# A new start for the first head pairs: P turned on VectorE, matrices built in halves, k and v in fp32 by SyncE, and a changed order of loads

## The chip, the cores and the metric

The kernel runs on one core of one Trainium2 chip. The metric is the device time of one execution in microseconds (us). Each run is repeated, and the mean TensorE clock that the core was granted is recorded with each execution.

A run also leaves a profile of one execution. Its span is about 2 us shorter than the device time, since it goes only from the first to the last instruction. Times inside a profile are counted from the start of its span. A load "lands" when its data has arrived.

## The reference

Attention over blocks comes first: a soft permutation P of the eight blocks of each head, found by five rounds of normalisation, sorts k and v. A feed-forward network (FFN) with a squared relu follows.

```python
batch, n_heads, seq, head_dim, n_blocks = 4, 8, 768, 64, 8
P = sort_net                                     # (4, 8, 8, 8)
for _ in range(5):
    P = exp(P - max(P, -1)); P /= sum(P, -1); P /= sum(P, -2)
k_sorted = einsum('bhij,bhjcd->bhicd', P, k in blocks of 96 rows)
v_sorted = einsum('bhij,bhjcd->bhicd', P, v in blocks of 96 rows)
attn = softmax(q_block @ k_sorted_block.T / 8)   # inside each block
x = (attn @ v_sorted).reshape(3072, 512)
out = maximum(x @ w_in, 0)**2 @ w_out            # 512 -> 2048 -> 512
```

## The kernel before

The kernel doesn't emit instructions as its source lists them. It collects operations (`plan.add(engine, estimated cost, function, dependencies)`) and a planner sorts them by the time at which each could start. Each engine then gets its own list and takes it strictly in order. That holds for the loads too: all loads that turn fp32 into bf16 are issued by GpSimd, one after another.

```python
    def dma(key, mb, dst_src, deps=(), long=True, rate=0.23):
        def issue(e):
            dst, src = dst_src()
            nc.gpsimd.dma_start(out=dst, in_=src)
        op = plan.add("POOL", 0.75, issue, deps)          # GpSimd
        landed[key] = plan.add("DMA", mb / (...), lambda e: None, [op, landed.get("last")])
        landed["last"] = landed[key]
    # [cut]
    for g in range(HP):                    # k and v of batch 0, pair of heads by pair
        load(0, 1, 2 * g, 2)
        load(0, 2, 2 * g, 2)
        if g == 0:
            plan.add("POOL", 1.5, make_mask, [id_op])
    load_w_in(0)
    for g in range(1, 4):
        load_w_in(g)
    load(1, 2, 0, HP)                      # "vb": the first half of v of batch 1
    for g in range(4):
        dma(("w_out", g), 1.05, ...)
    for t, g in ((2, 1), (1, 0), (0, 0), (1, 1), (0, 1)):
        load(1, t, HP * g, HP)
```

For the first pairs of batch 0, P is turned by a TensorE transpose, spread over the partitions by small matmuls, and multiplied with a mask on VectorE into the sorting matrices `w_all`. The start is then a fixed list of stages: K and V sort k and v of a pair, S computes scores, T turns v, A applies the attention, X turns the result into `xT` for the FFN.

```python
FIRST = ("K0 V0 K1 v1 S0 t0 S1 k2 t1 A0 V2 S2 K3 t2 A1 V3 X0 A2 S3 t3 x1 A3 X2 x3")
    # [cut]
    pe = plan.add("PE", 0.12, p_trans, [step] + old)
    op = plan.add("DVE", 0.18, lambda e: nc.vector.tensor_copy(out=p_ij, in_=tiles["pT"]), [pe])
    # [cut: spreading]
    build_w(2, 2, pt, cp)
    build_w(4, 4, pt, cp)
```

The softmax here doesn't subtract the row's maximum and nothing guards it: scores larger than these inputs give would overflow.

## Time and profile before

| | kernel before |
|---|---|
| time, median | 224.44 us (223.84 to 224.87, 4 runs) |
| span of the profile, mean clock | 222.0 us, 1.000 |
| TensorE, ScalarE, VectorE, GpSimd busy | 96%, 54%, 46%, 12% |
| first sort of a pair | 12.98 us |
| first FFN matmul | 22.48 us |
| first sort of vb, after 40 FFN matmuls | 30.34 us, no wait |
| second sort of vb | 42.89 us, 0.21 us of waiting |
| wait for vblk (v of a later batch, written to memory and read back) | 1.06 us, ending at 157.23 us |

Lines of a timeline read: start, duration, engine, source line, operation, output<-inputs, shape, count. In brackets stands how long the engine was idle before and what ended the idleness. The prediction shows the main lines of this profile.

### The profile page before, as it was taken

To read this page: it belongs to the slowest core of one execution; us is meant where nothing else is said; L and a number is where in the kernel's file an instruction comes from. 1 tells how busy PE (TensorE), PEld (TensorE's weight loads), DVE (VectorE), ACT (ScalarE), POOL (GpSimd) and SP (SyncE) were. 2 spreads that over 40 slices of the span, in tenths; PEclk is the share of its full clock that TensorE was granted. 3 is DMA by queue.
4 is the path that set the end of the run, shared out by engine and by line. 5 is a ranking of instruction groups with operands and counts; after the bars stand their busy time and mean duration, and the time that the engine had idled before them with its cause. 6 is when DMAs were issued, how large, how long until landed. Compare 5 with 4: busy or idle time off the path is not lost.

```text
span 222.0 us, 5101 instructions
## 1 busy us (share of the span) xinstructions
PE 213.3 (96%) x2049; PEld 120.0 (54%) x2065; DVE 102.8 (46%) x291; ACT 120.8 (54%) x249; POOL 26.5 (12%) x49
## 2 busy tenths in 40 slices
PE   8998999999999999999999999999899999999993
PEld 2576666456665555445665465445555465455562
DVE  6768477444773347602676056404655155015300
ACT  4666888217976168517864178329573276147421
POOL 7973230000000600000000240000000000000000
PEclk9999999999999999999999999999999999999999
DMA  5999999998533499189943599648982510120012
GB/s 68 201 202 207 209 206 214 209 259 229 156 82 80 90 227 223 25 218 223 206 111 83 120 176 218 128 139 177 238 175 68 118 49 3 47 94 0 3 63 78
DMA packets 46583, 31.22 MB, mean 141 GB/s; under 512 B 26016, under 2 KB 41632, under 8 KB 46560
## 3 DMA queue, kind: packets, MB, share of 16 engines
q0 software_dynamic: 12736, 13.63, 37.2%
q1 hardware_dynamic: 33824, 17.27, 30.8%
q8 instruction: 16, 0.26, 0.5%
q14 instruction: 7, 0.06, 0.1%
HBM read 29.70 MB, written 8.72 MB: 173 GB/s over the span
## 4 chain that ended last, share of the span: by engine, by line
PE 75%; DMA 17%; POOL 4%; ACT 1%; issue 1%; DVE 1%; SPq 0%; ACTq 0%
PE op L921 33%; PE hp L893 31%; DMA vb<-in_v_dram 9%; DMA w_in_bf<-in_moe_w_in_dram 5%; PE p L631 3%; PE p L814 3%; DMA vblk<-v_way 2%; PE op L955 2%; PE p L714 2%; POOL vb L300 1%; POOL kb L300 1%; DMA p_sb<-in_sort_net_dram 1%; ACT h L901 1%; DVE h L904 1%; PE qtp L511 0%
## 5 line engine op out<-in xcount | busy, mean ns | idle before, releaser
L893 PE MATMUL hp<-xT,w_in_bf 128*128 128x384 bf16 x512 | 88.9, 326 | 0.0
L921 PE MATMUL op<-w_out_bf,h 128*128 128x512 bf16 x352 | 83.3, 379 | 0.9 <-issue 0.2
L904 DVE TENSOR_TENSOR h<-h 128x384 bf16<-128x384 bf16 x128 | 44.5, 356 | 62.7 <-ACT h L901 62.3
L901 ACT ACTIVATE h<-hp 128x384 bf16<-128x384 f32 x128 | 61.6, 495 | 19.1 <-PE hp L893 15.6
L893 PEld LDWEIGHTS <-w_in_bf 128*128 128x128 bf16 x512 | 48.1, 98 | 32.1 <-issue 1.0
L921 PEld LDWEIGHTS <-h 128*128 128x128 bf16 x368 | 34.0, 98 | 37.6 <-issue 0.9
L229 ACT COPY ob<-op 128x512 f32<-128x512 f32 (+1 forms) x24 | 13.6, 567 | 62.4 <-PE op L921 59.8
L825 DVE TENSOR_TENSOR ao<-p,rec 96x512 bf16<-96x512 f32 x32 | 22.0, 687 | 1.2
L663 ACT ACTIVATE et<-p 96x384 bf16<-96x384 f32 x48 | 19.5, 489 | 3.1 <-PE p L631 3.1
L814 PEld LDWEIGHTS <-et 96*128 96x128 bf16 x256 | 11.3, 97 | 5.5 <-issue 1.7
L824 DVE RECIPROCAL rec<-p 96x8 f32<-96x8 f32 x32 | 6.4, 199 | 16.4 <-PE p L814 16.2
L1047 POOL COPY held<-xT 1x3 bf16<-1x3 bf16 (+1 forms) x2 | 0.4, 183 | 89.2 <-DMA xT<-ao 89.2
L397 PE MATMUL p<-ones 128*128 128x512 bf16 (+1 forms) x36 | 10.0, 399 | 1.1 <-DVE ones L250 1.1
L814 PE MATMUL p<-vblk,et 96*128 96x65 bf16 x192 | 8.9, 193 | 1.1 <-DMA vblk<-v_way 1.1
L231 DVE CAST vn<-p 128x768 bf16<-128x768 f32 x6 | 5.7, 958 | 8.5 <-PE p L714 8.5
L631 PEld LDWEIGHTS <-kx 64*128 64x128 bf16 x160 | 6.1, 156 | 3.9 <-issue 3.7
L631 PE MATMUL p<-qT,kx 64*128 64x96 bf16 x160 | 7.4, 228 | 0.0
L231 DVE CAST kn<-p 128x768 bf16<-128x768 f32 x5 | 4.8, 957 | 4.8 <-PE p L714 4.8
L300 POOL DMA_DIRECT2D kb<-in_k_dram x10 | 6.4, 643 | 3.5 <-DMA w_in_bf<-in_moe_w_in_dram 2.0
L300 POOL DMA_DIRECT2D qb<-in_q_dram x8 | 6.1, 770 | 4.9 <-DMA w_out_bf<-in_moe_w_out_dram 2.1
L300 POOL DMA_DIRECT2D vb<-in_v_dram x10 | 6.3, 628 | 3.3 <-DMA w_in_bf<-in_moe_w_in_dram 2.0
L654 ACT ACTIVATE et<-p 96x768 bf16<-96x768 f32 x8 | 6.2, 804 | 0.1
(80 smaller groups left out, 112.9 us busy)
## 6 DMA issues: line engine op xcount, KB each, us to landing
out_dram<-ob SPq DMA_DIRECT2D x23, 256.0 KB, 2.2
qb<-in_q_dram POOLq DMA_DIRECT2D x8, 384.0 KB, 11.0
v_way<-vn SPq DMA_DIRECT2D x6, 396.0 KB, 4.2
vblk<-v_way SPq DMA_DIRECT2D x6, 396.0 KB, 4.1
vb<-in_v_dram POOLq DMA_DIRECT2D x6, 384.0 KB, 11.4
kb<-in_k_dram POOLq DMA_DIRECT2D x6, 384.0 KB, 10.0
w_in_bf<-in_moe_w_in_dram POOLq DMA_DIRECT2D x4, 512.0 KB, 11.8
w_out_bf<-in_moe_w_out_dram POOLq DMA_DIRECT2D x4, 512.0 KB, 18.9
```

The source lines that it names most:

```text
L229: nc.scalar.copy(out=out, in_=in_)
L231: nc.vector.tensor_copy(out=out, in_=in_)
L300: nc.gpsimd.dma_start(out=dst, in_=src)
L397: nc.tensor.matmul(out=out, lhsT=ones, rhs=rhs, start=True, stop=True)
L631: nc.tensor.matmul(out=scp[:, h, BLK * n:BLK * (n + 1)], lhsT=(u.ksT[64 * h:64 * (h + 1), HS * hf + BLK * n:HS * hf + BLK * n + 128] if no ...
L663: nc.scalar.activation(out=et[:, h, 0:HS].rearrange("p (n c a) -> p n c a", c=C0, a=NA), in_=st["p"][0:96, h, 0:HS].rearrange("p (n a c) - ...
L814: nc.tensor.matmul(out=oup[:, h, 66 * n:66 * n + D + 1], lhsT=et_r[u.et[hf]][:, h, BLK * n:BLK * n + 128], rhs=(u.vs[:, NQ * hf + n, h, 0: ...
L825: nc.vector.tensor_tensor(out=u.ao[:, n0:n0 + NQ, :, :].rearrange("p n e d -> p e n d"), in0=ov[:, :, :, 0:D], in1=rec[:, :, :, None].to_b ...
L893: nc.tensor.matmul(out=t["hp", nt][:, 0:HS], lhsT=w_in_bf[:, kc, 128 * nt:128 * (nt + 1)], rhs=xT[:, kc, t0:t0 + HS], start=(kc == 0), sto ...
L901: nc.scalar.activation(out=t["h1", nt], in_=t["hp", nt][:, 0:HS], func=AF.Relu)
L904: nc.vector.tensor_tensor(out=t["h2"][:, nt, :], in0=t["h1", nt], in1=t["h1", nt], op=ALU.mult)
L921: nc.tensor.matmul(out=t["op", mt], lhsT=t["h2"][:, nt, 128 * mt:128 * (mt + 1)], rhs=w_out_bf[:, nt, :], start=(nt == 0), stop=(nt == NT ...
```

## The change

The intent is an earlier start. P takes a shorter way to the sorting matrices, the first matrix is built only as far as it is needed at once, the first k and v use DMA time that was idle, and nine FFN matmuls go one at a time into gaps of TensorE. To free VectorE, three builds move to GpSimd, and the later loads are put into a function that is called after the builds. One of them, vb, is given the last build as a dependency.

```diff
-FIRST = ("K0 V0 K1 v1 S0 t0 S1 k2 t1 A0 V2 S2 K3 t2 A1 V3 X0 A2 S3 t3 x1 A3 X2 x3")
+FIRST = ("K0' v0 k1 V1 S0 t0 v2 S1 t1' A0 K2' K3 V3 A1 t2 S2 x0' t3' S3 A2 F0 F1 X1' A3 X2' "
+         "F2 F4 F5 F3 x3 F6 F7 F8")
@@ loads
+    kv_f = xT[:, :, 3 * S:].bitcast(FP32).rearrange("p (t h) x -> p t h x", t=2)
+    for t, x in enumerate((k_r, v_r)):
+        nc.sync.dma_start(out=kv_f[:, t], in_=x[0, :, 0:2, :])
-    for g in range(HP):
+    plan.add("POOL", 1.5, make_mask, [id_op])
+    for g in range(1, HP):
         load(0, 1, 2 * g, 2)
         load(0, 2, 2 * g, 2)
-        if g == 0:
-            plan.add("POOL", 1.5, make_mask, [id_op])
-    load(1, 2, 0, HP)
-    for g in range(4):
-        dma(("w_out", g), ...)
+    def loads_after(deps):
+        load(1, 2, 0, HP, deps=deps)
+        for g in range(4):
+            dma(("w_out", g), ...)
@@ P
-        nc.tensor.transpose(
-            out=tiles["pT"], in_=pf.rearrange("h i j -> h (i j)"), identity=ident[0:NH, 0:NH])
+        nc.vector.transpose(out=p_ij.rearrange("p k h -> p (k h)"),
+                            in_=pf.rearrange("h i j -> h (i j)"))
@@ casts and builds
+    def cast(e, t):
+        nc.scalar.copy(out=qkv[0][t][:, 0:2, :], in_=kv_f[:, t - 1])
+    there = plan.add("WAY", 4.8, lambda e: None)
+    for t in (1, 2):
+        landed[0, t, 0, 0] = plan.add("ACT", 0.83, lambda e, t=t: cast(e, t), [there, exps[t]])
-    build_w(2, 2, pt, cp)
-    build_w(4, 4, pt, cp)
+    build_w(2, 2, pt, cp, 0, NQ)
+    builds = [build_w(h0, 4, pt, cp, i0, NQ, "POOL") for h0, i0 in ((4, 0), (0, NQ), (4, NQ))]
+    loads_after(builds[-1:])
@@ single FFN matmuls: stage F in FIRST
+        kc, nt = n // 3, n % 3
+        nc.tensor.matmul(
+            out=tiles["hp", nt][:, 0:HS], lhsT=w_in_bf[:, kc, 128 * nt:128 * (nt + 1)],
+            rhs=xT[:, kc, 0:HS], start=(kc == 0), stop=False)
[cut: the shapes for the turned P, the choice of PSUM buffers (the quote marks in FIRST), planning costs, fill sizes]
```

More of the change, by code (lines that the diff above doesn't have):

```diff
@@ L92 @@
 class Plan:
-    TAIL = {"PE": 0.0, "ACT": 0.09, "DVE": 0.06, "POOL": 0.0, "DMA": 0.0, "SP": 0.0, "WAY": 0.6}
+    TAIL = {"PE": 0.12, "ACT": 0.09, "DVE": 0.06, "POOL": 0.0, "DMA": 0.0, "SP": 0.0, "WAY": 0.6}
     HOP = 0.06
@@ L105, in add @@
     def add(self, eng, cost, fn, deps=(), due=0, ffn=False, mode="full"):
+        if eng == "PE":
+            cost += self.TAIL["PE"]
         op = Op(eng, cost, fn, deps, due, mode)
@@ L312, in in_tiles, with load @@
         return b > 1 and t > 0 or b == 1 and t == 2 or b == 1 and t == 1 and h0 == HP
-    def load(b, t, h0, n, p=slice(0, 128)):
+    def load(b, t, h0, n, p=slice(0, 128), deps=()):
         def dst_src():
@@ L321, in load @@
         dma((b, t, h0, p.start), 1.57 * n / H * (p.stop - p.start) / 128, dst_src,
-            readers[b - 2] + [holds[b]] if b > 1 else [],
+            readers[b - 2] + [holds[b]] if b > 1 else list(deps),
             b < 2 and (b < 1 or in_tiles(b, t, h0)), 0.23 if b == 1 else 0.37 if t else 0.29)
@@ L327, in load_w_in @@
         dma(("w_in", g), 1.05, lambda: (w_in_bf[:, :, f], w_in_r[:, :, f]))
-    first = plan.add("DMA", 4.3, lambda e: None)
+    first = plan.add("DMA", 4.8, lambda e: None)
     landed["last"] = first
@@ L356 @@
         load_w_in(g)
-    load(1, 2, 0, HP)
-    for g in range(4):
-        t = slice(NT // 4 * g, NT // 4 * (g + 1))
-        dma(("w_out", g), 1.05, lambda t=t: (w_out_bf[:, t, :], w_out_r[:, t, :]))
-    for t, g in ((2, 1), (1, 0), (0, 0), (1, 1), (0, 1)):
-        load(1, t, HP * g, HP)
+    def loads_after(deps):
+        load(1, 2, 0, HP, deps=deps)
+        for g in range(4):
+            t = slice(NT // 4 * g, NT // 4 * (g + 1))
+            dma(("w_out", g), 1.05, lambda t=t: (w_out_bf[:, t, :], w_out_r[:, t, :]))
+        for t, g in ((2, 1), (1, 0), (0, 0), (1, 1), (0, 1)):
+            load(1, t, HP * g, HP)
     rs = const.tile([NH, NB], FP32)
@@ L367 @@
     pf = const.tile([NH, NB, NB], BF16)
-    sel = const.tile([64, 64, C0], BF16)
+    sel = const.tile([32, 32, C0], BF16)
     pt = const.tile([128, NB, NH], BF16)
-    p_ij = const.tile([64, NH], BF16)
+    p_ij = const.tile([NH, 2, NH], BF16)
     def sink_norm(e, axis, last=False):
@@ L384, in make_sel @@
         nc.scalar.copy(
-            out=sel, in_=ident[0:64, 0:64, None].to_broadcast([64, 64, C0]))
+            out=sel, in_=ident[0:32, 0:32, None].to_broadcast([32, 32, C0]))
     tiles = {}
@@ L412, with p_turn @@
         if it == 0:
-            plan.add("ACT", 0.9, make_sel, [step, id_op])
+            plan.add("ACT", 0.6, make_sel, [step, id_op])
         step = plan.add("DVE", 0.66, lambda e: sink_norm(e, 0), [step])
         step = plan.add("DVE", 0.69, lambda e, it=it: sink_norm(e, 1, it == 4), [step])
-    def p_trans(e):
-        tiles["pT"] = ps1.tile([64, NH], BF16, tag="p1", name="pT")
-        nc.tensor.transpose(
-            out=tiles["pT"], in_=pf.rearrange("h i j -> h (i j)"), identity=ident[0:NH, 0:NH])
+    def p_turn(e):
+        nc.vector.transpose(out=p_ij.rearrange("p k h -> p (k h)"),
+                            in_=pf.rearrange("h i j -> h (i j)"))
     def p_spread(e, name, n):
@@ L428, in p_spread, with build_w @@
                 out=tiles[name][:, i, :],
-                lhsT=sel[:, NB * i:NB * (i + 1), :].rearrange("p j c -> p (j c)"),
-                rhs=p_ij[:, 0:n], start=True, stop=True)
+                lhsT=sel[:, NB * (i % 4):NB * (i % 4 + 1), :].rearrange("p j c -> p (j c)"),
+                rhs=p_ij[:, i // 4, 0:n], start=True, stop=True)
     built = {}
-    def build_w(h0, n, src, dep):
+    def build_w(h0, n, src, dep, i0=0, ni=NB, eng="DVE"):
+        i1 = slice(i0, i0 + ni)
         def fn(e):
-            s = tiles["pt_01"] if src is None else src
-            nc.vector.tensor_tensor(
-                out=w_all[:, h0:h0 + n, :, :],
+            (nc.vector if e == "DVE" else nc.gpsimd).tensor_tensor(
+                out=w_all[:, h0:h0 + n, i1, :],
                 in0=(mask if h0 < H else mask_1)[:, None, None, :]
-                .to_broadcast([128, n, NB, C0]),
-                in1=s[:, :, h0:h0 + n].rearrange("p i h -> p h i")[:, :, :, None]
-                .to_broadcast([128, n, NB, C0]),
+                .to_broadcast([128, n, ni, C0]),
+                in1=(tiles["pt_01"] if src is None else src)
+                [:, i1, h0:h0 + n].rearrange("p i h -> p h i")[:, :, :, None]
+                .to_broadcast([128, n, ni, C0]),
                 op=ALU.mult)
-        op = plan.add("DVE", 0.15 + 0.134 * n, fn, [dep])
+        cost = 0.15 + 0.134 * n * ni / NB if eng == "DVE" else 0.2 + 0.32 * n * ni / NB
+        op = plan.add(eng, cost, fn, [dep])
         for h in range(h0, h0 + n):
-            built[h] = op
+            for i in range(i0, i0 + ni):
+                built[h, i] = op
         return op
@@ L543, in s_q, with s_sort @@
         return op
-    def s_sort(u, t, due=0, early=False, eng=AD):
+    def s_sort(u, t, due=0, early=False, eng=AD, own=False):
         st = {}
@@ L551, in mm @@
             if early:
-                tp = psf.tile([128, 512], FP32, tag="pf", name="tp")
+                tp = ((ps1 if own else psf)
+                      .tile([128, 512], FP32, tag="p1" if own else "pf", name="tp"))
                 tp = tp[:, 0:NA * u.ni * C0].rearrange("p (a x) -> p a x", a=NA)
@@ L577, in s_sort @@
         dep = landed[u.b, t, h0 if u.b == 0 else HP * (h0 // HP), 0]
-        ring = rf if early else r2
+        ring = (r1 if own else rf) if early else r2
         s2, old = ring.take()
         pe = plan.add("PE", 0.336 if u.full else 0.2, mm,
-                      [dep, built[H * u.b + h0], built[H * u.b + h0 + 1]] + old, due, mode="col")
+                      [dep, built[H * u.b + h0, u.i0], built[H * u.b + h0 + 1, u.i0]] + old, due, mode="col")
         readers[u.b].append(pe)
@@ L608, in s_sort2 @@
         pes = [plan.add("PE", 0.2, lambda e, t=t: mm(e, t),
-                        [landed[u.b, t, 2 * u.hp, 0], built[H * u.b + 2 * u.hp],
-                         built[H * u.b + 2 * u.hp + 1]] + old, due, mode="col") for t in (1, 2)]
+                        [landed[u.b, t, 2 * u.hp, 0], built[H * u.b + 2 * u.hp, u.i0],
+                         built[H * u.b + 2 * u.hp + 1, u.i0]] + old, due, mode="col") for t in (1, 2)]
         readers[u.b] += pes
@@ L669, in s_sc, with s_vt @@
                 u.exps[hf].append(op)
-    def s_vt(u, due=0, eng=AD):
+    def s_vt(u, due=0, eng=AD, own=True):
         st = {}
+        ring = r1 if own else rf
         def mm(e):
-            st["p"] = vbp = ps1.tile([128, u.ni, 128], BF16, tag="p1", name="vbp")
+            st["p"] = vbp = ((ps1 if own else psf)
+                             .tile([128, u.ni, 128], BF16, tag="p1" if own else "pf", name="vbp"))
             for n in range(u.ni):
@@ L686, in ev @@
                  st["p"][0:96].rearrange("p n (e d) -> p n e d", d=D))
-        s1, old = r1.take()
+        s1, old = ring.take()
         pe = plan.add("PE", 0.446 if u.full else 0.22, mm, [u.v_op] + old, due)
         u.vs_op = one_of(eng, cost_b(128 * u.ni), ev, [pe] + u.old)
-        r1.use(s1, pe, u.vs_op)
+        ring.use(s1, pe, u.vs_op)
         rks.use(u.n, pe)
@@ L842, in s_av, with s_xt @@
         u.nao = nao
-    def s_xt(u, due=0, eng=AD):
+    def s_xt(u, due=0, eng=AD, own=True):
         if u.b > 1 or u.b == 1 and u.hp < HP - 1:
@@ L857, in s_xt @@
         st = {}
+        ring = r1 if own else rf
         def mm(e):
-            st["p"] = xtp = ps1.tile([128, u.ni, BLK], BF16, tag="p1", name="xtp")
+            st["p"] = xtp = ((ps1 if own else psf)
+                             .tile([128, u.ni, BLK], BF16, tag="p1" if own else "pf", name="xtp"))
             for n in range(u.ni):
@@ L869, in ev @@
             copy(e, xT[:, u.hp, t0:t0 + BLK * u.ni], st["p"].rearrange("p n q -> p (n q)"))
-        s1, old = r1.take()
+        s1, old = ring.take()
         pe = plan.add("PE", 0.342 if u.full else 0.17, mm, u.norms + old, due)
         op = one_of(eng, cost_b(BLK * u.ni), ev, [pe])
-        r1.use(s1, pe, op)
+        ring.use(s1, pe, op)
         rao.use(u.nao, pe)
@@ L877, in s_xt, with f_piece, mm @@
             x_done[u.b, u.hp, hf] = op
+    begun, f_slot = {}, {}
+    def f_piece(n):
+        kc, nt = n // 3, n % 3
+        def mm(e):
+            if kc == 0:
+                tiles["hp", nt] = psf.tile([128, 512], FP32, tag="pf", name="hp")
+            nc.tensor.matmul(
+                out=tiles["hp", nt][:, 0:HS], lhsT=w_in_bf[:, kc, 128 * nt:128 * (nt + 1)],
+                rhs=xT[:, kc, 0:HS], start=(kc == 0), stop=False)
+        old = begun.setdefault((0, nt), [])
+        if kc == 0:
+            f_slot[nt], old = rf.take()
+        pe = plan.add("PE", 0.163, mm, [x_done[0, kc, 0], landed["w_in", 0]] + old)
+        rf.use(f_slot[nt], pe)
+        begun[0, nt].append(pe)
     def ffn_unit(g):
@@ L890, in up @@
                     t["h2"] = ffn.tile([128, NT, HS], BF16, tag="h2", name="h2")
-                t["hp", nt] = psf.tile([128, 512], FP32, tag="pf", name="hp")
-                for kc in range(KC):
+                kcs = range(len(begun.get((g, nt), ())), KC)
+                if kcs[0] == 0:
+                    t["hp", nt] = psf.tile([128, 512], FP32, tag="pf", name="hp")
+                else:
+                    t["hp", nt] = tiles["hp", nt]
+                for kc in kcs:
                     nc.tensor.matmul(
@@ L905, in square @@
                     out=t["h2"][:, nt, :], in0=t["h1", nt], in1=t["h1", nt], op=ALU.mult)
-            sf, old = rf.take()
-            pe = plan.add("PE", 0.65, up, xs + [landed["w_in", nt // 4]] + old, ffn=True)
+            n = len(begun.get((g, nt), ()))
+            sf, old = rf.take() if n == 0 else (f_slot[nt], begun[g, nt])
+            pe = plan.add("PE", 0.65 * (KC - n) / KC, up, xs + [landed["w_in", nt // 4]] + old, ffn=True)
             s1, old1 = rh1.take()
@@ L976 @@
     q2ops = [s_q(0, hp, 64, 128, after=exps[4], eng="ACT") for hp in range(HP)]
-    s1, old = r1.take()
-    pe = plan.add("PE", 0.12, p_trans, [step] + old)
-    op = plan.add("DVE", 0.18, lambda e: nc.vector.tensor_copy(out=p_ij, in_=tiles["pT"]), [pe])
-    r1.use(s1, pe, op)
+    op = plan.add("DVE", 0.2, p_turn, [step])
     sf, old = rf.take()
     pe = plan.add("PE", 0.25, lambda e: p_spread(e, "pt_01", 2), [op] + old)
-    w0 = build_w(0, 2, None, pe)
+    w0 = build_w(0, 2, None, pe, 0, NQ)
     rf.use(sf, pe, w0)
@@ L997 @@
         stage = stage.upper()
+        if stage == "F":
+            f_piece(n)
+            continue
         if n not in us:
@@ L1001 @@
         u = us[n]
+        own = (name[2:] == "'") ^ (stage in "TX")
         if stage == "K":
-            u.k_op = s_sort(u, 1, early=True, eng=eng)
+            u.k_op = s_sort(u, 1, early=True, eng=eng, own=own)
         elif stage == "V":
-            u.v_op = s_sort(u, 2, early=True, eng=eng)
+            u.v_op = s_sort(u, 2, early=True, eng=eng, own=own)
         elif stage == "S":
@@ L1008 @@
         elif stage == "T":
-            s_vt(u, eng=eng)
+            s_vt(u, eng=eng, own=own)
         elif stage == "A":
@@ L1012 @@
         else:
-            s_xt(u, eng=eng)
+            s_xt(u, eng=eng, own=own)
     n_up = NT + 4 * (HS // 128)
@@ L1074 @@
             if filled and not started and op.gap > 0.15 and slot is not None:
-                fill(op.gap, slot)
+                fill(op.gap - 0.15, slot)
             filled = True
```

## The prediction

> **What bounds the kernel now.** I read the page first: engine shares, then the span in slices.
>
> ```profile
> PE 213.3 (96%) x2049; PEld 120.0 (54%) x2065; DVE 102.8 (46%) x291; ACT 120.8 (54%) x249; POOL 26.5 (12%) x49
> ...
> PE   8998999999999999999999999999899999999993
> ...
> DMA  5999999998533499189943599648982510120012
> ```
>
> TensorE is busy nearly throughout, so the work removed anywhere else is worth only what it lets TensorE start earlier. The third row shows a second limit: for the first nine slices (each 5.55 us) the DMA engines are full as well. In that stretch an early TensorE can run into data that has not come.
>
> Next the timeline of TensorE from 22 to 44 us:
>
> ```profile
> 22.48 0.34 PE L893 MATMUL hp<-xT,w_in_bf 128*128 128x384 bf16 x1
> ...
> 27.81 2.60 PE L893 MATMUL hp<-xT,w_in_bf 128*128 128x384 bf16 x15
> 30.34 0.38 PE L714 MATMUL p<-vb,w_t 32*32 32x384 bf16 x16
> 30.66 1.47 PE L893 MATMUL hp<-xT,w_in_bf 128*128 128x384 bf16 x8
> ...
> 42.89 0.39 PE L714 MATMUL p<-vb,w_t 32*32 32x384 bf16 x16 [0.21 <-DMA vb<-in_v_dram]
> ```
>
> The FFN begins at 22.48; what comes before is the start-up that the change rebuilds. At 30.34, after 40 FFN matmuls, TensorE sorts the first half of v of batch 1 (vb), at 42.89 the second half, which had only just landed. TensorE takes its list in order, so either sort can stop everything behind it.
>
> Last, the timeline of GpSimd, which issues all loads that cast:
>
> ```profile
> 10.42 3.04 POOL L300 DMA_DIRECT2D w_in_bf<-in_moe_w_in_dram  x4
> 14.81 0.55 POOL L300 DMA_DIRECT2D vb<-in_v_dram  x1 [1.35 <-DMA kb<-in_k_dram]
> 15.34 1.54 POOL L300 DMA_DIRECT2D w_out_bf<-in_moe_w_out_dram  x2
> 17.08 0.74 POOL L300 DMA_DIRECT2D w_out_bf<-in_moe_w_out_dram  x1 [0.20 <-issue]
> 19.63 0.74 POOL L300 DMA_DIRECT2D w_out_bf<-in_moe_w_out_dram  x1 [1.81 <-DMA w_in_bf<-in_moe_w_in_dram]
> 22.33 0.54 POOL L300 DMA_DIRECT2D vb<-in_v_dram  x1 [1.96 <-DMA w_in_bf<-in_moe_w_in_dram]
> ```
>
> Two things are to be seen. GpSimd idles before issues until an older load lands: in the program's list each such load waits for the one eight places before it. And vb, needed at 30.34, goes out ahead of all four parts of w_out, which are needed from 37.62 on. Adding the time to landing (view of the load line, one issue at a time) to the start gives the landings: k of pair 2 14.6, v of pair 2 14.9, k of pair 3 15.9, v of pair 3 16.8, the parts of w_in 19.3, 22.1, 24.6, 27.4, vb 28.9, w_out 31.5, 34.0, 37.0, 40.7, second vb 42.8. So vb is only 1.4 us early today, and a part of w_in or w_out takes about 2.6 us of a full DMA.
>
> **What the Trainium skill says.** "DMA: Bandwidth & Descriptors", section "Issuing engines are not separate DMA queues": loads issued by SyncE run on the same 16 engines. The trace agrees that only idle time can be won: the DMA share is 0.29 from 2 to 3 us and 0.84 from 3 to 4, then 1.31 from 5 to 15. The same page, "Two DMAs through the same engine are not ordered": descriptors of a queue start in order. The landings above are in issue order without exception. "GPSIMD Engine Reference", section "3.1 Elementwise — side-by-side cycle accounting": about 2.6 cycles an element against 1 on VectorE. The folds of the mask agree: 64 columns 0.34 us, 16 columns 0.22, so 2.5 ns a column. "TensorE: Matmul & The Clock Gate", section "What's actually happening": after an idle window of about 3.4 us the array runs at half clock until about 3.4 us of work. The trace shows the slow state at the start, where 12 filling matmuls of 512 columns take 5.30 us (0.44 each) against 0.82 for three later (0.27); PEclk doesn't show it.
>
> **The change part by part.**
>
> 1. P is turned on VectorE instead of by a TensorE transpose and a copy. Before: last write of P ends at 11.14, copy of the turned P ends at 11.90. After: one VectorE instruction on 32x64; small VectorE operations here take 0.17 to 0.25, so about 0.2 plus 0.05. Gain 0.5 us.
> 2. The first matrix is built for four of eight blocks. Three builds (256, 256, 512 columns) take 1.56; an estimate for 128 columns is 0.28 against 0.42. Gain 0.15. Pair 0 could be sorted at about 12.3 instead of 12.98.
> 3. k and v of pair 0 come in fp32 by SyncE from about 1.2 us and fill DMA time that was idle. Until 4.5 us the DMA moved 0.16 MB, where 0.2 MB/us is its later rate: about 1.2 us of idle time is filled, so all later landings come about 1.2 us earlier: k of pair 3 at 14.7, the last w_in at 26.2. ScalarE pays two casts of 128x768, 0.80 each by the casts of that shape here; they lie between the exponentials of P, which leave it idle 1.50 before the third.
> 4. Nine FFN matmuls (0.163 each, 1.47 in all) go into gaps of the last pairs, in place of filling matmuls.
> 5. The builds for pairs 2 and 3 move to GpSimd, and the vb load is made to wait for them. This is the part that decides. In the changed program GpSimd's list is: w_in x4, w_out x3, three builds, w_out, vb, vb. The third w_out waits for the eighth load before it, k of pair 3, about 14.7; with 0.74 of issue and a build of 256 columns (0.18 + 256 x 2.5 ns = 0.82) the sort of v of pair 2 starts at about 16.4.
>
> From 16.4 I follow the changed order by hand with durations of this trace: exponential of pair 1 ends 17.9 (0.81), three ScalarE evacuations of 0.48 to 19.4, two exponentials to 21.0, last normalisation (0.19 + 0.69) to 22.3, its transpose and copy (0.2 + 0.36) to about 22.9. At 22.9 nine FFN matmuls are done, so this equals a start at 21.4: a gain of 1.1 us over 22.48, although the first pair gained only 0.65.
>
> Then the loss. The first sort of vb stands behind 36 FFN matmuls instead of 40. From 22.48 to 30.34 there were 7.86 us with 40; with 27 left to do it is 7.86 - 13 x 0.163 = 5.7, so TensorE is there at about 28.6. The vb load is now behind four parts of w_out: 26.2 + 4 x 2.6 + 1.5 (vb's own time, 27.4 to 28.9) = 38.1. **TensorE waits 9.5 us**, with all later work behind it. The sort starts at 38.1 instead of 30.34: 7.8 later. Four more FFN matmuls are still to do: +0.65. The second vb lands at about 41.6, well before its sort, so the old wait there (0.2 to 0.4) goes: -0.3. After 9.5 us of idleness some 3.4 us of work at half clock lose about 1.5. Sum: 7.8 + 0.65 - 0.3 + 1.5 = +9.6 on TensorE's chain. From there to the end TensorE is full, so it goes through to the end: 224.6 + 9.6 = 234.2. I take 233.5, as small waits later (1.1 us for vblk near 157) may shrink and the clock loss is the softest term.
>
> **The rivals.** *The start-up gain comes through*: vb is there in time and the kernel ends 1 to 3 us sooner, 221.5 to 223.5. For it: the 1.1 us above. Against it: the order of loads is fixed in the program, and 4.2 MB at the measured 0.4 MB/us can't pass in the 2.4 us between 26.2 and 28.6. *GpSimd's builds become the bound instead*: if the third w_out is held longer or VectorE's two-input work slows the builds to 1.5 us each, pair 2 is sorted at 17.5 or later and the FFN starts later; but this only shortens the later wait for vb by as much, so the end moves little. *The casts hold up P*: if k of pair 0 lands after 5.0 us, the third exponential is late and all of the start-up with it. Likewise hidden behind vb. *The DMA is faster without the writes to v_way from 31.9 us on*: w_out parts took 3.0 and 3.7 us there and vb could land at 37: 1 us less, about 232.
>
> **Range and chances.** The landing of vb (36.5 to 40) gives 1.5 us each way, the clock 0 to 1.7, the changed order later 1 us each way: 229.5 to 237.5. Slower by over 2% means above 229.1. Even with vb at 36.5 and no clock loss the sum is +6.5, 231.1. Faster by 2% would need 220.1, more than the whole start-up gain: 0.02. Within 2% only if I misread the order: 0.06. Slower: 0.92.
>
> **What the changed profile would show.** Right: a TensorE gap of 8 to 10.5 us ending near 38 at the first sort of vb, put down to the DMA of vb; the fourth w_out issued before vb; first builds on GpSimd near 15.6; the first sort at about 12.3; slow matmuls just after the gap; about 1.1 us gained in FFN matmuls done by 22.9. Wrong: vb landing before 31, or FFN matmuls filling the gap, or GpSimd not waiting at the third w_out.

## The result, and the profile after

The changed kernel took 233.5 us (median, 233.46 to 234.2, 4 runs) against 224.44 us. The ratio is 1.041, with a 95% interval of 1.038 to 1.044: slower. Ratios here are the mean time of one kernel's runs over that of the other's runs of the same rounds, so not quite the ratio of the medians. The changed kernel's profiled span is 231.7 us, with a mean clock of 0.963.

The page of the changed kernel, engine shares and slices of 5.79 us:

```profile
PE 216.5 (93%) x2050; PEld 120.6 (52%) x2050; DVE 102.7 (44%) x292; ACT 121.0 (52%) x249; POOL 26.9 (12%) x50
...
PE   8699762999999999999999999999999999999993
...
PEclk9759995899999999999999999999999999999999
DMA  6999999964326149946994669937996520111012
```

TensorE has one new hole, the seventh slice (digit 2, 34.8 to 40.5 us) with two thinner ones ahead of it (7 and 6), and a thin second slice (digit 6). The clock row is down to 7 and 5 in the second and third slice, and to 5 and 8 in the hole and the slice after it. The DMA row is full right through the hole: the loads don't pause, they bring something else than what TensorE wants.

The timeline of TensorE around the hole, then that of GpSimd:

```profile
29.33 3.42 PE L931 MATMUL hp<-xT,w_in_bf 128*128 128x384 bf16 x20
38.97 0.55 PE L725 MATMUL p<-vb,w_t 32*32 32x384 bf16 x16 [6.21 <-DMA vb<-in_v_dram]
39.45 2.74 PE L931 MATMUL hp<-xT,w_in_bf 128*128 128x384 bf16 x8
...
52.44 0.38 PE L725 MATMUL p<-vb,w_t 32*32 32x384 bf16 x16
```

```profile
13.26 0.74 POOL L306 DMA_DIRECT2D w_out_bf<-in_moe_w_out_dram  x1 [0.23 <-DMA kb<-in_k_dram]
...
15.96 1.84 POOL L443 TENSOR_TENSOR w_all<-mask,pt 128x256 bf16<-128x256 bf16 x3
17.75 0.80 POOL L306 DMA_DIRECT2D w_out_bf<-in_moe_w_out_dram  x1
19.38 0.54 POOL L306 DMA_DIRECT2D vb<-in_v_dram  x1 [0.82 <-DMA w_in_bf<-in_moe_w_in_dram]
```

GpSimd issues three parts of w_out, the builds, the fourth part, and only then vb. TensorE is done with the work ahead of vb at 32.76 and stands for 6.21 us.

The chain of waits that ended last, its two longest early pieces:

```profile
8.98 10.11 DMA w_in_bf<-in_moe_w_in_dram
19.38 19.55 DMA vb<-in_v_dram
```

From 8.98 to 38.93 us the chain consists of transfers and of the issue between them. TensorE is nowhere on it in that time, so whatever the start-up won or lost in those 30 us isn't on the path that set the end.

That start-up did not go as intended. These lines are from the timelines of the kernel before (TensorE, ScalarE, VectorE), then of the changed one:

```profile
6.60 0.91 PE L511 MATMUL qtp<-ident,qb 64*64 64x64 bf16 x36 [0.24 <-DMA qb<-in_q_dram]
7.66 0.26 ACT L409 ACTIVATE p_sb<-p_sb 32x64 f32<-32x64 f32 x1
10.93 0.21 DVE L377 TENSOR_TENSOR pf<-p_sb,cs 32x64 bf16<-32x64 f32 x1
12.98 0.38 PE L560 MATMUL tp<-w_all,kb 128*64 128x64 bf16 x12 [0.25 <-ACT pt L988]
```

```profile
7.99 0.83 ACT L1013 CAST vb<-xT 128x768 bf16<-128x768 f32 x1 [1.69 <-DMA xT<-in_v_dram]
8.14 1.13 PE L519 MATMUL qtp<-ident,qb 64*64 64x64 bf16 x36 [2.05 <-DMA qb<-in_q_dram]
9.10 0.25 ACT L414 ACTIVATE p_sb<-p_sb 32x64 f32<-32x64 f32 x1
12.37 0.21 DVE L382 TENSOR_TENSOR pf<-p_sb,cs 32x64 bf16<-32x64 f32 x1
12.61 0.23 DVE L425 STREAM_TRANSPOSE p_ij<-pf 32x64 bf16<-32x64 bf16 x1
15.28 0.53 PE L569 MATMUL tp<-w_all,kb 128*64 128x64 bf16 x12 [0.22 <-DVE w_all L443]
```

The first q lands at about 8.1 instead of 6.5 us, the fourth exponential of P starts 1.44 us later, and the first sort comes at 15.28 instead of 12.98. Each matmul group of the last line also takes 0.53 instead of 0.38 us: TensorE runs at half clock there. The table of windows of the changed kernel shows where that began (columns: window, its length, then busy time of TensorE, its weight loads, VectorE, ScalarE, GpSimd, then clock, DMA share, GB/s):

```profile
6.00:8.00 2.00, 0.09 (x1) 0.00 (x0) 1.27 (x7) 0.27 (x2) 2.00 (x4) 1.00 1.27 224
8.00:10.00 2.00, 1.85 (x51) 1.53 (x51) 0.55 (x3) 2.00 (x5) 1.79 (x3) 0.56 1.31 202
...
16.00:18.00 2.00, 2.00 (x53) 1.59 (x48) 1.22 (x3) 1.50 (x3) 2.00 (x4) 0.50 1.25 206
```

So two causes offer themselves for the 9.7 us: the late vb, and the late start. The experiments part them.

### The profile page after: what moved, and what is told of

Same layout as the page of the kernel before. It is cut to its first block, busy times and chain, and to the rows that moved or that the text cites. A ratio compares the mean times of both kernels' runs of the same rounds, so it can differ in the third digit from the quotient of the medians.

```text
span 231.7 us, 5097 instructions
## 1 busy us (share of the span) xinstructions
PE 216.5 (93%) x2050; PEld 120.6 (52%) x2050; DVE 102.7 (44%) x292; ACT 121.0 (52%) x249; POOL 26.9 (12%) x50
## 4 chain that ended last, share of the span: by engine, by line
PE 79%; DMA 15%; POOL 3%; issue 1%; DVE 0%; ACT 0%; SPq 0%; POOLq 0%; ACTq 0%
PE op L960 34%; PE hp L931 33%; DMA vb<-in_v_dram 8%; DMA w_in_bf<-in_moe_w_in_dram 4%; PE p L825 3%; PE p L640 3%; DMA vblk<-v_way 2%; PE p L725 2%; PE op L994 2%; POOL kb L306 1%; POOL vb L306 1%; POOL qb L306 0%; PE xtp L876 0%; DVE vn L234 0%; PE p L605 0%
## 5 line engine op out<-in xcount | busy, mean ns | idle before, releaser
L960 PE MATMUL op<-w_out_bf,h 128*128 128x512 bf16 x368 | 84.9, 379 | 0.0
L939 ACT ACTIVATE h<-hp 128x384 bf16<-128x384 f32 x128 | 61.3, 495 | 20.2 <-PE hp L931 16.8
L931 PEld LDWEIGHTS <-w_in_bf 128*128 128x128 bf16 x503 | 47.4, 98 | 33.2 <-issue 3.1
L402 PE MATMUL p<-ones 128*128 128x512 bf16 (+1 forms) x22 | 8.5, 537 | 1.1 <-DVE ones L253 1.1
L725 PE MATMUL p<-vb,w_t 32*32 32x384 bf16 x96 | 2.7, 359 | 6.2 <-DMA vb<-in_v_dram 6.2
L232 ACT CAST vn<-p 128x768 bf16<-128x768 f32 x6 | 4.8, 799 | 6.8 <-PE p L725 6.8
L725 PEld LDWEIGHTS <-w_t 32*32 32x32 bf16 x176 | 1.7, 88 | 10.3 <-issue 9.8
```

The costliest lines, as they stand in the source:

```text
L232: nc.scalar.copy(out=out, in_=in_)
L402: nc.tensor.matmul(out=out, lhsT=ones, rhs=rhs, start=True, stop=True)
L725: nc.tensor.matmul(out=p2[slot][32 * c:32 * (c + 1), h, 0:NA * D], lhsT=w[r, :], rhs=src[r, g, NA * D * c:NA * D * (c + 1)], start=True, s ...
L931: nc.tensor.matmul(out=t["hp", nt][:, 0:HS], lhsT=w_in_bf[:, kc, 128 * nt:128 * (nt + 1)], rhs=xT[:, kc, t0:t0 + HS], start=(kc == 0), sto ...
L939: nc.scalar.activation(out=t["h1", nt], in_=t["hp", nt][:, 0:HS], func=AF.Relu)
L960: nc.tensor.matmul(out=t["op", mt], lhsT=t["h2"][:, nt, 128 * mt:128 * (mt + 1)], rhs=w_out_bf[:, nt, :], start=(nt == 0), stop=(nt == NT ...
```

## The experiments

Theory: the order in which GpSimd issues the loads, vb behind w_out, makes the whole loss, and the slower start is hidden behind it. Rival: the start (fp32 loads, casts, half clock) makes part of it. Each edit is against the changed kernel unless it says "before".

| run | median us | ratio to before, 95% | first sort | first sort of vb (wait) |
|---|---|---|---|---|
| after | 233.5 | 1.041 (1.038 to 1.044) | 15.28 | 38.97 (6.21) |
| e1 | 226.5 | 1.010 (1.006 to 1.015) | 13.25 | 34.15 (none) |
| e2 | 229.38 | 1.024 (1.018 to 1.031) | 12.20 | 34.13 (0.86) |
| e3 | 226.52 | 1.014 (1.006 to 1.021) | 12.20 | 31.72 (none) |
| e4 | 232.74 | 1.039 (1.034 to 1.044) | 12.76 | 37.04 (6.85) |
| e5 | 236.48 | 1.056 (1.052 to 1.061) | 12.20 | 39.27 (3.77) |
| e6 | 226.67 | 1.009 (1.002 to 1.015) | 12.43 | 31.16 (none) |
| e7 | 226.75 | 1.013 (1.007 to 1.018) | 15.66 | 33.33 (none) |
| e8 | 227.15 | 1.013 (1.008 to 1.018) | 15.33 | 33.57 (none) |
| e9 | 224.6 | 1.003 (0.999 to 1.007) | 12.67 | 30.24 (none) |
| e10 | 227.68 | 1.014 (1.010 to 1.018) | 12.41 | 29.23 (none) |

The first two number columns are over 4 executions of the kernel named (6 for e5, e9 and e10), compared with 4 to 11 of the kernel before from the same rounds. The last two come from one profiled execution each, and such a reading scatters: up to its first sort e4 has the instructions of the kernel before, and it sorts at 12.76 where that one sorts at 12.98.

### e1: vb doesn't wait for the builds

```diff
-        load(1, 2, 0, HP, deps=deps)
+        load(1, 2, 0, HP)
```

> The changed kernel with one edit: the load of the first half of v of batch 1 (vb) no longer waits for the builds on GpSimd, so it is issued ahead of all four w_out loads; the lists of the other engines are the same instruction for instruction. Theory 1 (load order: the wait for vb sets the end): vb lands at 28.5 instead of 38.97, TensorE is at its sort at 32.8 and doesn't wait; 6.2 us of wait and about 1.3 us of half clock after it go, so 233.5 - 7.5 = 226.0 (225.3 to 227). Rival, theory 2 (the slow start-up is what costs 9 us): 231 or more.

Only GpSimd's list changes: vb is issued at 12.97 us, ahead of every part of w_out. The time falls to 226.5 us, as expected, and the first sort of vb follows on without a wait:

```profile
34.15 0.38 PE L725 MATMUL p<-vb,w_t 32*32 32x384 bf16 x16
```

One argument in one line carries 7.0 of the 9.1 us. About 2.3 us over the kernel before remain. In this profile the slower start is now uncovered: TensorE reaches this sort 3.8 us later than the kernel before. Part of this is a wait of 1.76 us for GpSimd's builds, which in this run stand behind vb and two parts of w_out; another part is half clock from about 13 to 23 us. That the start makes all of the remaining 2.3 us isn't shown: e3 below, with the start repaired, has the same median (226.52).

### e4: the kernel before, with vb late

```diff
 before
-    load(1, 2, 0, HP)
-    [the other later loads]
+    def loads_after(deps):
+        load(1, 2, 0, HP, deps=deps)
+        [the other later loads]
 [cut]
-    build_w(4, 4, pt, cp)
+    w3 = build_w(4, 4, pt, cp)
+    loads_after([w3])
```

> The kernel before with the one dependence put in: its first vb load waits for the last build of the first matrices, which puts it behind three w_out loads on GpSimd; the lists of all other engines are the same as before. Theory 1: vb lands at about 28.9 + 3 x 2.6 = 36.7, TensorE waits from 30.3 to 36.7 and then runs some us at half clock: 224.4 + 6.4 - 0.3 + 1.3 = 231.8 (230.5 to 233). Theory 2: the start-up is untouched, so 224 to 225.

This is the counterpart: all that was new in the start is missing, and only the dependency is added to the kernel before. The lists of all engines but GpSimd stay as they were. It takes 232.74 us:

```profile
37.04 0.55 PE L715 MATMUL p<-vb,w_t 32*32 32x384 bf16 x16 [6.85 <-DMA vb<-in_v_dram]
```

Here vb stands behind three parts of w_out, where the changed kernel has it behind four. The late vb alone makes 3.9% of the 4.1%. Together with e1 this settles the main cause: taking it away from the changed kernel takes most of the loss away, and putting it into the kernel before makes nearly all of it.

### e2: k and v of pair 0 by GpSimd again

```diff
-    kv_f = xT[:, :, 3 * S:].bitcast(FP32).rearrange("p (t h) x -> p t h x", t=2)
-    for t, x in enumerate((k_r, v_r)):
-        nc.sync.dma_start(out=kv_f[:, t], in_=x[0, :, 0:2, :])
-    first = plan.add("DMA", 4.8, lambda e: None)
+    first = plan.add("DMA", 4.3, lambda e: None)
-    for g in range(1, HP):
+    for g in range(HP):
[and without the two casts]
```

> The changed kernel with the first k and v loaded and cast by GpSimd as in the kernel before; no fp32 loads by SyncE and no casts on ScalarE. The load order stays as changed (vb behind three w_out). Theory 1: the start-up recovers (last write of P at about 11.2 instead of 12.58, no half clock from 8 to 19.7, FFN some 3 us sooner), but the wait for vb grows by as much, and the end stays: 233.5 (232.5 to 234.5). Theory 2: the loss falls with the start-up, to about 228 or less.

A miss: 229.38 us. The expectation rested on the order of loads staying as it was, and it didn't: with other start times, the planner put vb ahead of the last two parts of w_out. So the run mixes two causes and says little about the end. It does show the start by itself. Without the fp32 loads the first sort comes at 12.20, where the prediction had 12.3 for the changed kernel. The short way of P and the half builds thus gain 0.78 us over the kernel before; with the scatter (12.76 in e4 for the old start, 12.41 and 12.43 in e10 and e6 for this one) it may be as little as 0.35. The fp32 loads cost 3.08 us in the profile of the changed kernel (15.28). In e1, whose start has the same instructions, they cost 1.05 (13.25): there q landed a little earlier, TensorE idled 1.04 instead of 2.05 us before it, and the clock didn't fall until about 13 us. The last write of P ends at 11.07 in e2, 12.12 in e1 and 12.58 in the changed kernel; the first sort follows 1.13, 1.13 and 2.70 us later. So about 1.5 us of the 3.08 is a later P. The other 1.6 come behind P, where TensorE, at half clock since about 8.2 us, still has transposes of q and filling matmuls ahead of the spreading (14.46, no idle before it).

### e5: e2 with the order of loads forced back

```diff
 e2
[cut: a dict, issues, that keeps the issue of each load]
+    done = plan.run()
+    for op in [issues["w_out", g] for g in (0, 1, 2)]:
+        done.remove(op); done.insert(done.index(builds[0]), op)
+    vb_op = issues[1, 2, 0, 0]
+    done.remove(vb_op)
+    done.insert(done.index(issues["w_out", 3]) + 1, vb_op)
```

> The clean form of e2, whose load order had shifted too (vb went behind one w_out before the builds and one after, and landed near 34). Here first k and v come by GpSimd as in e2 and the lists of TensorE, ScalarE and VectorE are those of e2, but GpSimd's list is w_out x3, builds, w_out, vb, vb as in the changed kernel. Theory 1 (the landing of vb sets the end, the start-up is hidden behind it): TensorE is at the vb sort near 34 and waits to 39.5: 234 (233 to 235.5). Theory 2 (the slow start-up costs): 229 to 230 like e2.

Here GpSimd's list is that of the changed kernel again (w_out three times, builds, w_out, vb), and the start is the good one of e2. If the start mattered behind a late vb, the time would fall. It rose to 236.48 us (234.19 to 237.07). The rival's 230 or less is out, though the median also lies above the expected range; the profiled execution, at 234.19 us, lies in it. Two waits of TensorE:

```profile
17.81 0.53 PE L568 MATMUL tp<-w_all,vb 128*64 128x64 bf16 x12 [3.58 <-POOL w_all L442]
...
39.27 0.39 PE L724 MATMUL p<-vb,w_t 32*32 32x384 bf16 x16 [3.77 <-DMA vb<-in_v_dram]
```

The 3.08 us of earlier start were first spent on waiting for GpSimd's builds, which stand behind three issues of w_out, and then vb landed no earlier than in the changed kernel. Why the other five executions took longer than the profiled one, one of them by 0.7 us and four by 2.3 to 2.9, isn't shown; their clocks were lower (0.963 to 0.970 against 0.975).

The changed kernel's own four executions point the same way. Their mean clocks were 0.963, 0.978, 0.969 and 0.963, while their times were 233.46, 233.51, 233.49 and 234.2 us. A mean clock lower by 0.015 means 0.015 x 231.7 / 0.5 = 7 us more at half clock, and between the first two executions that moved the time by 0.05 us. Only one of them was traced, so whether those 7 us lay in the start or in the hole isn't shown.

### e3: both edits

```diff
[e1 and e2 together]
```

> Both edits at once: vb not waiting for the builds and the first k, v by GpSimd. Theory 1: neither the wait nor the slow start is left; what remains is the turned P, the half builds, the builds on GpSimd, the single FFN matmuls and the new order: the first sort at about 12.4 instead of 12.98, about 1 us gained in the FFN's start: 223.5 (222.3 to 224.8). Theory 2 expects the same of this run; it differs in e1 and e2.

A miss by 3 us: 226.52 us, where the repaired start should have beaten the kernel before. vb is sorted at 31.72, 1.4 us after the kernel before, although the first sort is 0.78 us earlier. Three waits lie between that the kernel before doesn't have: 0.90 us for the builds on GpSimd (the sort of v of pair 2), 0.57 us for x turned by ScalarE, and 0.69 us for a relu on ScalarE. The last comes from the nine single matmuls: they hold the three PSUM buffers (where matmul results collect) with half-finished FFN tiles, so the fourth tile has to wait until one of them is emptied. In this profile the clock is also at half from about 12.2 to 15.6 us. Further on, the second half of vb is sorted at 43.90 instead of 42.89, and the wait for vblk (explained under e10) is 1.79 instead of 1.06 us: 1.7 us together, where the spans differ by 1.6 (223.6 against 222.0).

### e6: e3 with all later loads behind the builds

```diff
 e3
-            dma(("w_out", g), 1.05, lambda t=t: (w_out_bf[:, t, :], w_out_r[:, t, :]))
+            dma(("w_out", g), 1.05, lambda t=t: (w_out_bf[:, t, :], w_out_r[:, t, :]), deps)
-            load(1, t, HP * g, HP)
+            load(1, t, HP * g, HP, deps=deps)
[vb keeps its deps here]
```

> e3 with one edit: all later loads wait for the builds, so GpSimd's list is w_in x4, builds x3, vb, w_out x4, vb; the lists of the other engines are the same as in e3. If the builds standing behind a load issue (15.28) cost e3 its gain, they now start near 12.5 and the sort of v of pair 2 waits for its data alone, about 15.0 instead of 15.99: 226.5 - 1.0 = 225.5 (224.5 to 226.3). If the F matmuls and their PSUM banks cost it, no change: 226.5.

The builds now start at 13.85 us, not as early as expected: the issue of the fourth part of w_in ahead of them had waited until 13.09 for an older load to land. The wait for the builds is gone, but the time, 226.67 us, is that of e3. The two ScalarE waits are still there:

```profile
22.00 0.81 PE L900 MATMUL hp<-xT,w_in_bf 128*128 128x384 bf16 x4 [0.57 <-ACT xT L232]
...
25.26 0.81 PE L928 MATMUL hp<-xT,w_in_bf 128*128 128x384 bf16 x4 [0.69 <-ACT h L936]
```

### e10: e6 without the nine single matmuls

```diff
 e6
-FIRST = ("... S3 A2 F0 F1 X1' A3 X2' F2 F4 F5 F3 x3 F6 F7 F8")
+FIRST = ("... S3 A2 X1' A3 X2' x3")
```

> The kernel of e6 (k and v of pair 0 by GpSimd, all later loads after the builds) without the nine single FFN matmuls; the FFN begins only after the last pair. Theory: the single matmuls hold the three PSUM banks and cost e6 the two waits 0.57 (for x turned) and 0.69 (for the relu), 1.26 us, against 1.47 us of FFN work done early in gaps that are partly filled anyway. If the gaps were real idle time, taking them away costs; if they stood on the path, it gains. I expect both waits to go and the time within 1 us of e6: 225.7 to 227. Rival: the waits are what keeps these kernels above the one before, and then this one falls to 224.5 to 225.3.

Both ScalarE waits vanish as expected, yet the time is 227.68 us, above the expected range. vb is sorted at 29.23 us after 32 FFN matmuls; the eight that e6 had done more would take 8 x 0.163 = 1.3 us, so this equals 30.5 against 31.16 in e6 and 30.34 in the kernel before. The 0.6 us won is lost again further on, where two later loads set the pace. The second half of vb and vblk, the v of a later batch that goes out to memory and back:

```profile
43.03 0.39 PE L721 MATMUL p<-vb,w_t 32*32 32x384 bf16 x16 [0.83 <-DMA vb<-in_v_dram]
...
159.51 0.66 PE L821 MATMUL p<-vblk,et 96*128 96x65 bf16 x16 [2.11 <-DMA vblk<-v_way]
```

The kernel before sorts the second half of vb at 42.89. TensorE in e10 has fewer FFN matmuls behind it and is 1.1 us ahead at the first sort, but it meets the same landing at 43.0, so the work that it left for later isn't repaid. And the wait for vblk is 1.05 us longer, after which the clock is at 0.58 and 0.56 in the windows from 160 to 164 us. The 16 FFN matmuls there take 4.44 us, against 2.76 at the same place in the kernel before. e6 shows the same drop from 159 to 163 us after a wait of 1.81 us; e3, with 1.79 us, and the kernel before, with 1.06 us, don't.

### e7 and e8: the fp32 loads kept, the start repaired in another way

```diff
 e7: the order of loads as in e6, fp32 loads kept, and
-        landed[0, t, 0, 0] = plan.add("ACT", 0.83, lambda e, t=t: cast(e, t), [there, exps[t]])
+        landed[0, t, 0, 0] = plan.add("ACT", 0.83, lambda e, t=t: cast(e, t), [there, exps[4 if t == 2 else t]])
 e8: e7, and
-        fill(3.5, 0)
+        fill(6.5, 0)
```

> The changed kernel with SyncE's fp32 k and v kept, all later loads after the builds, and the cast of v on ScalarE moved behind the last exponential of P. If the cast held up P (ScalarE waited 1.69 us for v, the fourth exponential came at 9.10), the last write of P goes from 12.58 back to about 11.2; the half clock from 8 us on stays, as q still lands near 8.1: 225.0 (224 to 226.5). Were P held up by something else, P stays at 12.5 and the time near 226.

> e7 with nine more filling matmuls at the start (19 instead of 10 in the first fill), so that TensorE isn't idle from 6.1 to 8.1 us. If that idle time is what put the clock to half until about 19.7, the clock stays at 1.00, sorts of the first pairs take 0.38 instead of 0.53 and the time falls by 1 to 2 us: 223.5 (222.3 to 224.8), level with the kernel before or just under. If the half clock comes from something else: 225 as e7.

Both miss. I had taken the cast of v, for which ScalarE waits 1.69 us in the changed kernel, for what holds up P, and the idleness before q for what lowers the clock. With the cast moved behind the last exponential (e7) the first sort stays late, at 15.66. With more filling matmuls (e8), which end at 7.58 us and still leave TensorE idle for 1.21 us before q, the clock holds 1.00 until about 10.7 us and then falls to half anyway, until 21 us. The timeline of ScalarE in e8 shows what P waits for once the cast is gone:

```profile
9.20 0.48 ACT L232 COPY qT<-qtp 128x384 bf16<-128x384 bf16 x1 [2.90 <-PE qtp L519]
```

In ScalarE's list a copy of q stands before the fourth exponential, and it waits for q, which is late itself. What is common to the changed kernel, e7 and e8 is the late q; in e2, e3 and e6, where SyncE's fp32 loads are gone, the first sort is early. So the fp32 loads can hold up P in two ways, by the cast and by the displaced q, and with the cast removed (e7) q is left. The other half, q in time and the cast left, wasn't run. Why the clock falls in e8 after no longer idleness than that is open.

### e9: the kernel before, with P turned by VectorE alone

```diff
 before
-    pe = plan.add("PE", 0.12, p_trans, [step] + old)
-    op = plan.add("DVE", 0.18, lambda e: nc.vector.tensor_copy(out=p_ij, in_=tiles["pT"]), [pe])
+    op = plan.add("DVE", 0.2, p_turn, [step])
```

> The kernel before with one part of the change alone: P is turned by one VectorE instruction instead of a TensorE transpose and a VectorE copy. All lists of instructions are otherwise the same (the fills of gaps differ by a few). Theory: the start-up gains what the prediction gave this part, 0.5 us: first sort at about 12.4 instead of 12.98. The landings don't move, so v of pair 3 (16.8) and the loads of w_in may give part of it back; the first sort of vb (30.34 before) would come at 29.8 to 30.3, still after vb's landing at 28.9. Time 0.2 to 0.5 us under the kernel before: 223.7 to 224.0. Rival: the whole start-up is bound by the loads, so that an earlier P buys nothing and the time is that of the kernel before, 224.2.

The part costs nothing and gains nothing that the runs can tell: 224.6 against 223.9 us, interval 0.999 to 1.007. The first sort moves by 0.31 us (12.98 to 12.67), the first FFN matmul by 0.11, the first sort of vb by 0.10 (30.34 to 30.24). Against e4, which has the old start too (first sort 12.76, first FFN matmul 22.25), it is 0.09 earlier and then 0.12 later, so a gain isn't clear of the scatter. After that there is a wait that the kernel before doesn't have:

```profile
41.23 1.89 PE L920 MATMUL op<-w_out_bf,h 128*128 128x512 bf16 x8 [0.47 <-DMA w_out_bf<-in_moe_w_out_dram]
```

The expected 0.2 to 0.5 us did not show. In this profile TensorE runs into the last part of w_out at 41 us, and the wait for vblk is 1.7 instead of 1.06 us. No version found here beats the kernel before. The six changed versions in which vb is in time (e1, e3, e6, e7, e8, e10) have medians of 226.5 to 227.7, with a good start or a bad one. What costs these 2 to 4 us was not isolated, and the half builds and the builds on GpSimd weren't run alone.

## Why the prediction was right, and where it was not

**The end and its cause were right; the exact hit was luck.** Predicted 233.5, measured 233.5 us, though the terms below missed in both directions. The list of GpSimd is as it was read from the program: builds at 15.96 (predicted 15.6), vb behind four parts of w_out. vb is sorted at 38.97 (predicted landing 38.1), put down to its DMA, with slow matmuls after it: eight FFN matmuls take 2.74 instead of 1.47 us, a loss of 1.27 (predicted 1.5). e1 and e4 show that the late vb is the cause.

**The sum, with measured terms.** vb is sorted 8.63 us later than before (predicted 7.8), four more FFN matmuls remain (0.65, counted as predicted), the half clock costs 1.27, the wait at the second vb goes (-0.21), and the vblk wait shrinks from 1.06 to 0.47 (-0.59). This makes 9.75; the spans differ by 9.7. The waits for vblk, before and after:

```profile
157.23 0.66 PE L814 MATMUL p<-vblk,et 96*128 96x65 bf16 x16 [1.06 <-DMA vblk<-v_way]
```

```profile
167.21 0.66 PE L825 MATMUL p<-vblk,et 96*128 96x65 bf16 x16 [0.47 <-DMA vblk<-v_way]
```

vb came 0.8 later than predicted; this was balanced by the vblk wait, which the prediction allowed for only roughly, and by the clock term.

**The step "a gain of 1.1 us at the start" failed**, and with it "TensorE is there at about 28.6" and "waits 9.5 us". TensorE arrived at 32.76 and waited 6.21. The start lost about 3 us (32.76 against 30.34 with four FFN matmuls fewer done, 2.4 + 0.65) instead of gaining 1.1. The number hardly felt it, because all of it lay ahead of the wait. Two terms of it were wrong:

- *"fill DMA time that was idle ... all later landings come about 1.2 us earlier"* was mis-sized. DMA shares summed second by second from 2 to 8 us are 0.29 + 0.84 + 1.19 + 1.34 + 1.29 + 1.34 = 6.29 before and 0.60 + 1.26 + 0.97 + 1.16 + 1.22 + 1.32 = 6.53 after. The idle time was used from 2 to 4 us, but from 4 to 6 us, where GpSimd now made its masks before it issued more, the DMA was less full than before. By the shares the net is only 0.24 / 1.3, about 0.2 us of a full DMA. The landings moved by more than that and by less than 1.2: k of pair 3 came at 15.0 instead of 15.9, v of pair 3 at 16.9 instead of 16.8, the last w_in at 26.7 (12.29 + 14.4) instead of 27.4, where 26.2 was predicted. Of the 0.8 us by which vb came late, this is 0.5; vb's own time, 1.9 instead of 1.5, is the rest.
- *"they lie between the exponentials of P"* was wrong. v in fp32 landed at 8.0 us (issued at 1.67, 6.3 to landing), and ScalarE, waiting in order for its cast, held the fourth exponential. The rival "the casts hold up P" named this; it had put the condition on k (in by 4.4, in time), where v was the late one. That q would be pushed back by the fp32 loads, from 6.5 to 8.1 us, and hold P as well (e8), was not foreseen. Half clock over the whole start, 8.2 to 18.5 us, was not in the prediction either.

**The terms for P itself:** the turn takes 0.23 us (predicted 0.2); its gain alone was 0.1 to 0.3 us (e9, measured against e4 and the kernel before) against 0.5, and together with the half builds 0.35 to 0.78 us (e2) against 0.65. Three builds on GpSimd took 1.84 us, 0.61 each, where the slope of the mask folds had given 0.82: beyond the fixed 0.18 that the prediction took, 1.7 ns a column and not 2.5. In the prediction's hand count to 22.9, the step from 21.0 to 22.3 names 0.88 us of normalisation; the other 0.4 aren't named.

**The nine single matmuls** were booked as work moved into gaps. They also bring two waits of 1.26 us together (e6, e10). At the first sort of vb this is a net loss of about 0.6 us, though without them the whole kernel was no faster (227.68 against 226.67).

**The rival "the start-up gain comes through"** was rightly put aside, but for one reason more than it gave: even with vb in time, the last part of w_out (e9) and the second vb (e10) hold TensorE at 41 to 43 us. The kernel before already stood at that limit: its own chain that ended last runs over the transfer of the second vb (22.33 to 42.84 us), so a start that is only earlier has nothing to gain up to there.

## What to carry to other kernels

A dependency added to a load can move it behind loads that have none, as here behind four parts of w_out; where one engine issues loads in order, read the issue order that comes out of the planner, not the order in the source, and ask of each load when its reader comes. A wait that ends on a transfer hides all that is upstream, gains and losses alike: take that wait out first (e1), or put it alone into the old kernel (e4), before judging the other parts. Idle DMA time filled by an early load isn't free when another load, here q, was to land soon after.

## What the Trainium skill lacked or had wrong

- "TensorE: Matmul & The Clock Gate", section "What's actually happening", puts the fall to half clock after an idle window of about 3.4 us and the return after about 3.4 us of sustained work, with a window that runs freely and isn't tied to the kernel. The lengths agree: read in windows of 1 us, the stretches at half clock last 3.4 us (e2, e3, e6, e10), 6.8 us (the changed kernel from 35.5 to 42.4, e5, which has one of 3.4 as well) or 10.2 us (the changed kernel from 8.2 to 18.5, e1, e4, e7, e8), so once, twice or three times 3.4. Two things don't agree. No wholly idle window was needed: 2.05 us of idleness (to 8.14 us) were enough in the changed kernel, and in e2 the clock fell at 17.1 us, after a wait of 1.97 us that had ended at 16.20. And the return took longer than that much work: in the changed kernel the clock stayed at 0.50 until 18.5 us, although matmuls filled 1.78 to 2.00 us of each 2 from 8 us on, and in e4 it came back 5.7 us after TensorE had restarted (37.04 to 42.7). No run here isolates what the gate counts as busy.
- "VectorE: DVE Perf Modes", section "The three transpose paths", times only the 128x128 case. Here a 32x64 bf16 transpose on VectorE took 0.23 us.
- "DMA: Bandwidth & Descriptors", section "Issuing engines are not separate DMA queues" (used in the prediction), says that loads of SyncE and GpSimd run interleaved on the same DMA engines. What no page that I read gives is a number for how far a plain fp32 load holds up a casting load beside it. Here 384 KB of k in fp32 took 3.2 us from issue to landing, the same amount of v 6.3 us, and the casting load of q beside them landed 1.6 us later than without them.
